# One number for a step's kind, read at the step's begin, in an attention and expert-routing kernel

## The chip, the cores and the metric

The kernel runs on one core of one Trainium2 chip. The metric is the device time of one execution in microseconds (us). The runs before the change took 690.76, 691.85 and 693.32 us, a median of 691.85 us.

A core has five engines that run their own instruction streams and meet at semaphores: PE (TensorE, the matmuls), DVE (VectorE), ACT (ScalarE), POOL (GpSimd) and SP (SyncE, which issues most transfers). A branch on a value that the kernel computed needs the value in a register of each engine that branches: the engine's stream holds an instruction TENSOR_LOAD that reads it from SBUF, and a compare-and-branch that uses it.

## The reference

A linear attention with random features over 8 batches of 576 tokens and 8 heads gives a matrix x of 4608 rows and 512 columns. Each row is then sent to one of 8 experts:

```python
logits = x @ w_gate
expert_idx = np.argmax(logits, axis=1)
...
for e in range(E):
    mask = expert_idx == e
    xe = x[mask]
    h = np.maximum(xe @ w1[e], 0.0)
    ye = h @ w2[e]
    out[mask] = gate_w[mask, None] * ye
```

`w1[e]` is 512 by 1024, `w2[e]` is 1024 by 512, all in float32. How many rows an expert gets is known only on the chip.

## The kernel before

The first 262 us or so are the attention. Its rows go to a buffer `token_rows` in HBM, and tables of row numbers are worked out on the chip (`slots`). `plan` (30-odd small DVE instructions on one partition) then fills `flags`, a table of integers with one column for a step: row 0 says that the expert changes, row 1 which expert to load next, row 2 that the step exists, row 4 that its second tile exists, and before the change row 5 that it has two tiles of 128 rows (a pair) and row 6 that its third tile has at most 64 rows (half).

The experts' part runs in steps. A step takes up to three tiles of 128 rows of one expert. Its rows are gathered from `token_rows` (`gather`, `gather3`: POOL), transposed by a transfer (`flips`, `flips3`: SP), put together as floats on ACT (`join`) and split in a high and a low part, `xh` by ACT and `xl` by DVE (`split_columns`). The first layer, `l1`, has three bodies of code: 256 columns for a pair, 320 where the third tile is half, 384 else. It stands twice, for the two halves of the hidden columns (`part` 0 and 1), and each half begins with the branches on the step's kind. A body makes groups of matmuls into a PSUM tile `p` (L1030); ACT writes `hh` from each (L1044) and DVE `hl` (L1045). The second layer, `l2`, multiplies `hh` and `hl` by the split `w2` (L1064 to L1066) for two or three tiles into `p_t`, `p_snu` and `p_skv`; `send` scales a tile with its gate on ACT and DVE (L1077, L1078), and POOL writes its rows out (L1079).

The order on each engine is the order in which the code is written (no scheduler moves it). In `step(t)` that is: `flips` of step t+1, the split of a new `w2` where the expert changes, `l1(t)`, the gathers of step t+2, the two loads of the kind of step t+1 (`kind`, by `reg` at L959: two on PE, DVE and ACT, one on POOL), `following`, and `l2(t)`. `following` is `begin(t+1)`: `xtrans` joins and splits the two tiles of the next step, `third` the third one, if the step is no pair (the branch at L1020 on `two`), and `change` splits a new `w1`. Steps from the 13th on stand in `tail`, nested, each under a branch on row 2.

A step begins with the first matmul of l1 on PE and has two borders there: from l1 to l2, where the two loads of the next step's kind stand, and from l2 to the next step's l1, where before the change there are branches alone (in `tail` the load of row 2, `v`, as well). The first step is led in by hand: the first two tiles of the table (`idx0`) are done in plain float32 by `l20(0)` and `l20(1)` (L933, into `p_snu` and `p_t`), and the kind of step 1 is loaded between those two.

```python
kind = self.kind(1)
self.third(kind[0])
...
self.l20(1)
...
for t in range(1, NPM - 1):
    kind = self.step(t, kind, ...)
```

Of the kernel before, what the change touches and what calls it, by code (L numbers as in the profile page):

```python
# [11 lines left out]
I32 = mybir.dt.int32  # L12
# [3 lines left out]
ALU = mybir.AluOpType  # L16
# [18 lines left out]
NPR = NPL + E - 1  # L35
NS = 3 * NPR
NPM = (NT // P - E) // 2
# [4 lines left out]
ET = mybir.EngineType  # L42
# [426 lines left out]
class Routing:  # L469
# [256 lines left out]
    def slots(self, wk, T1, banks, idx, fill, ahead):  # L726
# [14 lines left out]
        for c in (c1, c2, ch):  # L741
# [15 lines left out]
        nc.vector.scalar_tensor_tensor(out=v, in0=off, scalar=256.0, in1=m, op0=ALU.mult, op1=ALU.add)  # L757
        so, rt = self.L.rearrange("p g s e -> p (g s) e"), self.RT.rearrange("p g s -> p (g s)")
        y, tt, mv, sx, d, third, far = (t(n, [P, NLT]) for n in ("y", "tt", "mv", "sx", "d", "third", "far"))
        nc.vector.tensor_tensor(out=so, in0=self.OH.rearrange("p g s e -> p (g s) e"),  # L760
                                in1=v.unsqueeze(1).to_broadcast([P, NLT, E]), op=ALU.mult)
# [6 lines left out]
        nc.vector.scalar_tensor_tensor(out=d, in0=sx, scalar=64.0, in1=d, op0=ALU.mult, op1=ALU.add)  # L768
        nc.vector.scalar_tensor_tensor(out=mv, in0=d, scalar=-2.5, in1=sx, op0=ALU.is_gt, op1=ALU.mult)
        nc.vector.scalar_tensor_tensor(out=third, in0=d, scalar=-3.0, in1=sx, op0=ALU.is_equal, op1=ALU.mult)  # L770
        nc.vector.tensor_tensor(out=tt, in0=tt, in1=mv, op=ALU.subtract)
        nc.vector.scalar_tensor_tensor(out=third, in0=d, scalar=0.0, in1=third, op0=ALU.is_equal, op1=ALU.add)
# [22 lines left out]
    def plan(self, flags):  # L795


        nc, t, inc = self.nc, self.t, self.inc
# [20 lines left out]
        nt, en, sb = t("nt", [1, NQ]), t("en", [1, E]), t("sb", [1, NQ])  # L819
# [9 lines left out]
        sx, hf, two, thr = (t(n, [1, NQ]) for n in ("psx", "hf", "two", "thr"))  # L829
# [5 lines left out]
        nc.vector.scalar_tensor_tensor(out=two, in0=sb, scalar=4.0, in1=two, op0=ALU.is_equal, op1=ALU.add)  # L835
        nc.vector.tensor_tensor(out=two, in0=two, in1=sx, op=ALU.mult)
        nc.vector.scalar_tensor_tensor(out=two, in0=sb, scalar=3.0, in1=two, op0=ALU.is_equal, op1=ALU.add)
        nc.vector.tensor_single_scalar(flags[:, 5, :], two, 0.5, op=ALU.is_lt)
        nc.vector.scalar_tensor_tensor(out=flags[:, 6, :], in0=sb, scalar=5.0, in1=hf, op0=ALU.is_lt, op1=ALU.mult)
        nc.vector.tensor_single_scalar(flags[:, 4, :], sb, 1.5, op=ALU.is_gt)  # L840
        for i, a in ((0, ch), (1, nt), (2, act)):
            nc.vector.tensor_copy(flags[:, i, :], a)
# [2 lines left out]
class Experts:  # L845
# [6 lines left out]
    def __init__(self, tc, ctx, rt, xs, w1, w2, out, ident, ps):  # L852
        self.tc, self.nc, self.ctx, self.rt, self.ps, self.ident = tc, tc.nc, ctx, rt, ps, ident
        self.xs16, self.w1, self.w2, self.out = xs.bitcast(U16), w1, w2, out
        cp = ctx.enter_context(tc.tile_pool(name="mo_a", bufs=1))
        self.w1s = cp.tile([P, self.NC, F], F32, name="w1s")
        self.w2s = cp.tile([P, self.NF, DM], F32, name="w2s")
        self.idx = cp.tile([P, NS], U32, name="idx")
        self.x0 = cp.tile([P, self.NC, self.T2], F32, name="x0")
        self.idx0 = cp.tile([P, 2], U32, name="idx0")  # L860
        self.flags = cp.tile([1, 7, NPR + 2], I32, name="flags")
        self.xg = [cp.tile([P, 2 * ROW], U16, name=f"xg{i}") for i in range(2)]
        for x in self.xg:
            self.nc.gpsimd.memset(x, 0)
        rt.setup()
        rt.after[3] = rt.head(4, self.idx0, self.flags)
        gt = cp.tile([P, 8], F32, name="gt")
        self.gt = [gt[:, i:i + 1] for i in range(8)]
# [98 lines left out]
    def split(self, n, cs=range(8)):  # L967
        for c in cs:
            split_r(self.nc, *self.part(n, c), self.nc.scalar, self.nc.vector)
# [42 lines left out]
            self.split_columns(a, xw)  # L1012

    def flips3(self, t):
        with self.tc.If(self.reg(5, t, 1, (ET.SP,)) < 1):
            self.flip(self.xt3, self.x3)
        self.nc.gpsimd.tensor_copy(self.gt[6 + t % 2], self.gate(self.x3))

    def third(self, two):
        with self.tc.If(two < 1):  # L1020
            self.join(self.xw[0], self.xt3)
            self.split_columns(2, self.xw[0])

# [21 lines left out]
            self.nc.vector.scalar_tensor_tensor(out=b, in0=o, scalar=0.0, in1=a.bitcast(F32), op0=ALU.max,  # L1045
                                                op1=ALU.subtract)

    def l1(self, t, two, half):

        for part in range(2):  # L1050
            with self.tc.If(two > 0) as pair:
                self.layer(t, part, self.T2)
            with pair.Else():
                with self.tc.If(half > 0) as short:
                    self.layer(t, part, self.T2 + P // 2)
                with short.Else():
                    self.layer(t, part, self.T3)
# [36 lines left out]
        e = self.reg(1, t, E - 1, (ET.SP,))  # L1094
        (self.dma1 if n == 1 else self.dma2)(bass.ds(e, 1))

    def begin(self, t, kind):

        self.xtrans(t)
        self.third(kind[0])  # L1100
        self.change(t, 1)

    def kind(self, t):
        engines = (ET.PE, ET.DVE, ET.Activation, ET.Pool)
        return self.reg(5, t, 1, engines), self.reg(6, t, 1, engines[:3])

    def step(self, t, kind, following, split=lambda: None):
        engines = (ET.PE, ET.DVE, ET.Activation, ET.Pool)
        if t + 1 < NPR:
            self.flips(t + 1)  # L1110
            self.flips3(t + 1)
        split()
        two, half = kind
        self.l1(t, two, half)
        if t + 2 < NPR:
            self.gather(t + 2)
            self.gather3(t + 2)
        if t == 1:
            self.next(0, 2)
        kind1 = self.kind(t + 1) if t + 1 < NPR else None  # L1120
        following(kind1)
        self.nc.gpsimd.drain()
        with self.tc.If(two > 0) as pair:
            self.l2(t, 0)
            self.when(self.reg(4, t, 1, engines), lambda: self.l2(t, 1))
        with pair.Else():
            for a in range(3):
                self.l2(t, a)
        return kind1

    def tail(self, t, kind):
        split = lambda: self.change(t, 2)
        if t == NPR - 1:
            self.step(t, kind, lambda kind: None, split)
            return
        v = self.reg(2, t + 1, 1, (ET.PE, ET.DVE, ET.Activation, ET.SP, ET.Pool))
        kind = self.step(t, kind, lambda kind: self.when(v, lambda: self.begin(t + 1, kind)), split)
        with self.tc.If(v > 0):  # L1138
            self.tail(t + 1, kind)

    def run(self, ctx):
        nc, rt = self.nc, self.rt
        cp = ctx.enter_context(self.tc.tile_pool(name="mo_c", bufs=1))
        NC, NF, T2 = self.NC, self.NF, self.T2
        one, two = (self.ps.tile([P, 512], F32, name=f"p_s{g}", tag=g) for g in ("nu", "kv"))
# [35 lines left out]
        self.next(0, 1)  # L1181
        self.gather3(1)
        self.flips3(1)
        kind = self.kind(1)
        self.third(kind[0])
        self.gather(2)
        self.gather3(2)
        self.l20(1)
        self.hh, self.hl = held("hh"), held("hl")
        for t in range(1, NPM - 1):  # L1190
            kind = self.step(t, kind, lambda kind: self.begin(t + 1, kind), lambda: self.change(t, 2) if t > 1 else None)
        self.tail(NPM - 1, kind)


def attention_moe(tc, q, k, v, omega, wg, w1, w2, out, xs):
# [41 lines left out]
```

## Time and profile before

| what | value |
|---|---|
| runs, median | 690.76, 691.85, 693.32 us; 691.85 us |
| the profiled execution's own time | 687.46 us |
| its span, first to last instruction | 685.7 us |
| granted TensorE clock, mean | 0.997 |
| busy: PE, weight loads, ACT, DVE, POOL | 94%, 85%, 61%, 50%, 40% |
| steps of the experts' part | 15, the first matmul at 280.53, the last at 678.67 us |

The profile is of one execution. Times in its rows count from the first instruction. Register loads, branches and semaphore instructions are not in the rows as busy: what they cost is seen only as a time in which an engine begins its next instruction later than the one before would let it. A matmul row's duration overlaps the next row's (the matmuls are pipelined), so what a row takes of PE's time is the distance from its start to the next start.

### The profile page before, as it was taken

How to read it: one execution, taken by the hardware profiler on the slowest of the kernel's cores; microseconds unless marked ns; L12 is line 12 of the kernel's file. 1: busy time of each engine (PE TensorE's matmuls, PEld its weight loads, DVE VectorE, ACT ScalarE, POOL GpSimd, SP SyncE). 2: the span in 40 equal slices, each digit the busy share in tenths (PEclk: the TensorE clock that was granted, in tenths of full speed). 3: DMA queues.
4: the chain of work that ended last, by engine and by line, in shares of the span. 5: the costliest groups of instructions: out<-in, count | busy, mean ns of one | idle time of the engine just before them, and what ended most of it. 6: DMA issues, size and time to landing. Idle time of an engine off the chain costs nothing. (4 is left out here: it accounts for less than half of the span.)

```text
span 685.7 us, 19398 instructions
## 1 busy us (share of the span) xinstructions
PE 647.6 (94%) x7209; PEld 585.0 (85%) x7209; DVE 344.7 (50%) x800; ACT 416.3 (61%) x1037; POOL 277.7 (40%) x499
## 2 busy tenths in 40 slices
PE   6899999899899897999999999999999999999996
PEld 5788989889898884788998989988988989989894
DVE  3467979879888888622222245222245254222220
ACT  6999999999999986433424256134256264343320
POOL 8566767667668832523230303321203303312211
PEclk9999999999999999999999999999999999999998
DMA  7865475654834532694350119543219508732101
GB/s 214 223 193 163 120 211 152 198 155 128 233 118 157 179 90 62 213 208 126 86 111 17 64 48 290 128 72 74 64 56 267 145 6 278 191 68 50 43 8 38
DMA packets 113336, 89.93 MB, mean 131 GB/s; under 512 B 72222, under 2 KB 96798, under 8 KB 113184
## 3 DMA queue, kind: packets, MB, share of 16 engines
q1 hardware_dynamic: 105360, 68.78, 38.0%
q0 software_dynamic: 7280, 19.04, 8.2%
q8 instruction: 90, 1.47, 0.9%
q14 instruction: 62, 0.51, 0.3%
q10 hardware_dynamic: 544, 0.13, 0.1%
HBM read 63.46 MB, written 19.55 MB: 121 GB/s over the span
## 5 line engine op out<-in xcount | busy, mean ns | idle before, releaser
L1030 PE MATMUL p<-xh,w1p 128*128 128x256 f32 (+2 forms) x960 | 147.8, 296 | 0.0
L1079 POOL DMA_INDIRECT out_dram<-ys,idx x32 | 33.6, 1050 | 270.4 <-DVE ys L1078 194.2
L1030 PEld LDWEIGHTS p<-xh,w1p 128*128 128x128 f32 x960 | 135.3, 188 | 1.7 <-issue 0.5
L1044 ACT ACTIVATE hh<-p 128x384 fp32r<-128x384 f32 (+1 forms) x84 | 45.0, 537 | 131.2 <-PE p L1030 119.5
L1045 DVE SCALAR_TENSOR_TENSOR hl<-p,hh 128x384 fp32r<-128x384 f32 (+1 forms) x84 | 51.4, 614 | 122.8 <-ACT hh L1044 108.9
L233 ACT ACTIVATE qp<-pp,mx 128x128 f32<-128x128 f32 x256 | 94.6, 714 | 0.0
L233 ACT ACTIVATE kp<-pp,mx 128x128 f32<-128x128 f32 x256 | 92.2, 672 | 0.5 <-DVE mx L221 0.2
L221 DVE TENSOR_REDUCE mx<-pp 128x8 f32<-128x1024 f32 x64 | 78.0, 1219 | 26.2 <-PE pp L214 25.7
L1030 PE MATMUL p<-xl,w1p 128*128 128x256 f32 (+2 forms) x480 | 83.5, 296 | 0.0
L192 ACT COPY tq<-tt 128x1024 f32<-128x1024 f32 x59 | 81.5, 1381 | 0.9 <-PE tt L150 0.9
L214 PE MATMUL pp<-om_t,tq 64*128 64x128 f32 x1024 | 74.3, 284 | 2.6 <-ACT qp L233 1.7
L1030 PEld LDWEIGHTS p<-xl,w1p 128*128 128x128 f32 x480 | 70.5, 188 | 0.2 <-issue 0.2
L249 POOL TENSOR_TENSOR k<-kp 128x256 f32<-128x256 f32 x64 | 46.4, 725 | 54.0 <-ACT kp L233 50.4
L214 PEld LDWEIGHTS pp<-om_t,tq 64*128 64x128 f32 x1024 | 62.1, 187 | 6.3 <-ACT qp L233 3.2
L1004 ACT COPY xw<-xt 128x1024 uint16<-128x1024 uint16 x36 | 48.7, 1353 | 7.6 <-ACT hh L1044 4.5
L1064 PE MATMUL p_t<-w2p,hh 128*128 128x512 f32 x120 | 47.9, 399 | 4.4 <-ACT hh L1044 3.0
L48 DVE TENSOR_TENSOR xl<-xw,xh 128x512 fp32r<-128x512 f32 x36 | 24.8, 692 | 50.2 <-ACT xh L54 40.5
L305 PE MATMUL nu<-kva,tq 128*64 128x73 f32 x992 | 42.4, 230 | 5.4 <-ACT kva L292 5.4
L1065 PE MATMUL p_t<-w2p,hh 128*128 128x512 f32 x120 | 46.9, 391 | 0.3 <-issue 0.3
L1066 PE MATMUL p_t<-w2p,hl 128*128 128x512 f32 x120 | 47.1, 392 | 0.0
L1066 PE MATMUL p_snu<-w2p,hl 128*128 128x512 f32 x120 | 47.0, 391 | 0.0
L1064 PE MATMUL p_snu<-w2p,hh 128*128 128x512 f32 x120 | 47.0, 391 | 0.0
(395 smaller groups left out, 1281.3 us busy)
## 6 DMA issues: line engine op xcount, KB each, us to landing
w1s<-in_moe_w_dram SPq DMA_DIRECT2D x5, 2048.0 KB
w2s<-in_moe_w_dram SPq DMA_DIRECT2D x5, 2048.0 KB, 10.2
v<-in_v_dram SPq DMA_DIRECT2D x32, 256.0 KB, 3.5
token_rows<-xc SPq DMA_DIRECT2D x8, 1024.0 KB
k<-in_k_dram SPq DMA_DIRECT2D x31, 256.0 KB, 5.2
q<-in_q_dram SPq DMA_DIRECT2D x31, 256.0 KB, 5.6
kr<-in_k_dram SPq DMA_DIRECT2D x16, 64.0 KB, 3.7
vz<-in_v_dram SPq DMA_DIRECT2D x16, 64.0 KB, 2.4
```

The source lines that it names most:

```text
L192: self.nc.scalar.copy(self.pack(i, j), tt)
L214: nc.tensor.matmul(pp[:, a, n, i, :], th[r, k].rearrange("p a t -> p (a t)"), self.om[r, :], start=True, stop=True)
L221: nc.vector.tensor_reduce(out=mx[:, :, n], in_=s[("pp", h)][:, :, n], axis=AX.X, op=ALU.max, negate=True)
L233: nc.scalar.activation(x[:, j, :], pp[:, j % 2, n, j // 2, :], AF.Exp, bias=mx[:, j % 2, n, j // 2:j // 2 + 1])
L249: add = lambda o, x, y: nc.gpsimd.tensor_tensor(out=o, in0=x, in1=y, op=ALU.add)
L1004: self.nc.scalar.copy(x.bitcast(U16).rearrange("p c (t k) -> p k c t", k=2), xt.rearrange("p (k c) t -> p k c t", k=2))
L1030: self.nc.tensor.matmul(o, w[:, i, c], x[:, i, :], start=k == 0, stop=k == len(ops) - 1)
L1044: self.nc.scalar.activation(a, o, AF.Relu)
L1045: self.nc.vector.scalar_tensor_tensor(out=b, in0=o, scalar=0.0, in1=a.bitcast(F32), op0=ALU.max, op1=ALU.subtract)
L1064: nc.tensor.matmul(p, h, self.w2h[:, c, :], start=c == 0, stop=False)
L1065: nc.tensor.matmul(p, h, self.w2l[:, c, :], start=False, stop=False)
L1066: nc.tensor.matmul(p, l, self.w2h[:, c, :], start=False, stop=c == self.NF - 1)
```

## The change

The kind becomes one number in row 5: 2 for a pair, 1 for a half third tile, 0 else. It is loaded at three places, each time anew: by PE, DVE, ACT and POOL right before `l1(t)` (also used by the branch of `l2(t)`), by ACT and DVE in `third`, and by SP in `flips3` as before. The two loads between l1 and l2 are gone, and `third` is no branch of PE and POOL any more. `plan` has one instruction more.

```diff
-        nc.vector.tensor_single_scalar(flags[:, 5, :], two, 0.5, op=ALU.is_lt)
-        nc.vector.scalar_tensor_tensor(out=flags[:, 6, :], in0=sb, scalar=5.0, in1=hf, op0=ALU.is_lt, op1=ALU.mult)
+        nc.vector.scalar_tensor_tensor(out=hf, in0=sb, scalar=5.0, in1=hf, op0=ALU.is_lt, op1=ALU.mult)
+        nc.vector.tensor_scalar(out=two, in0=two, scalar1=-2.0, scalar2=2.0, op0=ALU.mult, op1=ALU.add)
+        nc.vector.tensor_tensor(out=flags[:, 5, :], in0=two, in1=hf, op=ALU.max)
...
-        self.flags = cp.tile([1, 7, NPR + 2], I32, name="flags")
+        self.flags = cp.tile([1, 6, NPR + 2], I32, name="flags")
...
-        with self.tc.If(self.reg(5, t, 1, (ET.SP,)) < 1):
+        with self.tc.If(self.kind(t, (ET.SP,)) < 2):
...
-    def third(self, two):
-        with self.tc.If(two < 1):
+    def third(self, t):
+        with self.tc.If(self.kind(t, (ET.DVE, ET.Activation)) < 2):
...
-            with self.tc.If(two > 0) as pair:
+            with self.tc.If(kind > 1) as pair:
                 self.layer(t, part, self.T2)
             with pair.Else():
-                with self.tc.If(half > 0) as short:
+                with self.tc.If(kind > 0) as short:
...
-    def kind(self, t):
-        engines = (ET.PE, ET.DVE, ET.Activation, ET.Pool)
-        return self.reg(5, t, 1, engines), self.reg(6, t, 1, engines[:3])
+    def kind(self, t, engines):
+        return self.reg(5, t, 2, engines)
...
         split()
-        two, half = kind
-        self.l1(t, two, half)
+        kind = self.kind(t, engines)
+        self.l1(t, kind)
...
-        kind1 = self.kind(t + 1) if t + 1 < NPR else None
-        following(kind1)
+        following()
         self.nc.gpsimd.drain()
-        with self.tc.If(two > 0) as pair:
+        with self.tc.If(kind > 1) as pair:
...
-        kind = self.kind(1)
-        self.third(kind[0])
+        self.third(1)
         self.gather(2)
         self.gather3(2)
         self.l20(1)
```

On PE, at the lead-in, before the change (`p_snu` is l20(0), `p_t` l20(1), `p<-xh,w1p` the first matmul of step 1):

```order
L933 MATMUL p_snu<-w2s,h_5983 128x512 x8
L959 TENSOR_LOAD flags
L959 ISA x2
L959 TENSOR_LOAD flags
L959 ISA x2
L1015 UNCONDITIONAL_BRANCH
L1020 COMPARE_AND_BRANCH
L1020 UNCONDITIONAL_BRANCH x2
L933 MATMUL p_t_5896<-w2s,h_5983 128x512 x3
L1015 UNCONDITIONAL_BRANCH
L933 MATMUL p_t_5896<-w2s,h_5983 128x512 x5
L1051 COMPARE_AND_BRANCH
```

The same place on PE in the changed kernel:

```order
L934 MATMUL p_snu<-w2s,h_5983 128x512 x8
L934 MATMUL p_t_5896<-w2s,h_5983 128x512 x8
L960 TENSOR_LOAD flags
L960 ISA x2
L1016 UNCONDITIONAL_BRANCH
L1021 UNCONDITIONAL_BRANCH
L1016 UNCONDITIONAL_BRANCH
L1052 COMPARE_AND_BRANCH
L1031 MATMUL p_5716<-xh,w1p_5723 128x256
```

The load has moved from between l20(0) and l20(1) to behind both, and there is one instead of two.

On PE, the border from l1 to l2 of step 1, before the change (the last matmuls of the 384 body, then the first of l2):

```order
L1030 MATMUL p_5719<-xl,w1p_5723 128x384 x4
L1054 UNCONDITIONAL_BRANCH
L959 TENSOR_LOAD flags
L959 ISA x2
L959 TENSOR_LOAD flags
L959 ISA x2
L1020 COMPARE_AND_BRANCH
L1020 UNCONDITIONAL_BRANCH x2
L1084 UNCONDITIONAL_BRANCH
L1123 COMPARE_AND_BRANCH
L1064 MATMUL p_t_5896<-w2p_5980,hh 128x512
```

In the changed kernel this border, with the border from l2 to the next step's l1 below it (from `p_skv` on):

```order
L1031 MATMUL p_5719<-xl,w1p_5723 128x384 x4
L1055 UNCONDITIONAL_BRANCH
L1021 UNCONDITIONAL_BRANCH
L1085 UNCONDITIONAL_BRANCH
L1122 COMPARE_AND_BRANCH
L1065 MATMUL p_t_5896<-w2p_5980,hh 128x512
...
L1067 MATMUL p_skv<-w2p_5980,hl 128x512
L1122 UNCONDITIONAL_BRANCH
L960 TENSOR_LOAD flags
L960 ISA x2
L1016 UNCONDITIONAL_BRANCH
L1085 UNCONDITIONAL_BRANCH
L1052 COMPARE_AND_BRANCH
```

The first border has lost both loads and one compare-and-branch; the second, which held two unconditional branches and the compare-and-branch, has got one load.

## Rows read from the trace of the kernel before

**Rows 1.** Groups by form on PE, 262 to 686: count | busy, mean | idle before

```profile
L1030 PE MATMUL p<-xh,w1p 128*128 128x256 f32 x576 | 78.2, 278 | 0.0
...
L1030 PE MATMUL p<-xh,w1p 128*128 128x384 f32 x192 | 37.5, 337 | 0.0
L1030 PE MATMUL p<-xh,w1p 128*128 128x320 f32 x192 | 32.0, 309 | 0.0
```

**Rows 2.** Waits of PE, 260 to 686: total us, times, longest

```profile
PE p_t L933 <- DVE w1p L48: 3.5, 1, 3.5
PE p_t L1064 <- ACT hh L1044: 3.0, 3, 1.2
PE p_t L1064 <- issue: 1.0, 3, 0.5
```

**Rows 3.** Timeline of PE, the lead-in: start us, duration us, instruction, count [idle before]

```profile
263.37 7.11 PE L933 MATMUL p_snu<-w2s,h 128*128 128x512 f32 x16
273.96 7.13 PE L933 MATMUL p_t<-w2s,h 128*128 128x512 f32 x16 [3.48 <-DVE w1p L48]
280.53 0.68 PE L1030 MATMUL p<-xh,w1p 128*128 128x256 f32 x1
```

**Rows 4.** Timeline of DVE at the same time

```profile
272.28 0.16 DVE L842 CAST flags<-f_act 1x27 int32<-1x27 f32 x1
272.36 2.48 DVE L48 TENSOR_TENSOR w1p<-w1s,w1p 128x512 fp32r<-128x512 f32 x4
...
275.17 1.27 DVE L48 TENSOR_TENSOR xl<-xw,xh 128x512 fp32r<-128x512 f32 x2
276.37 2.48 DVE L48 TENSOR_TENSOR w1p<-w1s,w1p 128x512 fp32r<-128x512 f32 x4
```

**Rows 5.** Timeline of PE, a pair's l1: between its halves, and its end

```profile
330.89 0.62 PE L1030 MATMUL p<-xl,w1p 128*128 128x256 f32 x4
331.34 1.07 PE L1030 MATMUL p<-xh,w1p 128*128 128x256 f32 x8
...
336.33 0.62 PE L1030 MATMUL p<-xl,w1p 128*128 128x256 f32 x4
336.98 0.47 PE L1064 MATMUL p_t<-w2p,hh 128*128 128x512 f32 x1
```

**Rows 6.** Timeline of PE, l1 to l2 of a 384 step and a 320 step

```profile
364.39 0.86 PE L1030 MATMUL p<-xl,w1p 128*128 128x384 f32 x4
365.09 0.39 PE L1064 MATMUL p_t<-w2p,hh 128*128 128x512 f32 x1
...
395.38 0.75 PE L1030 MATMUL p<-xl,w1p 128*128 128x320 f32 x4
396.20 0.47 PE L1064 MATMUL p_t<-w2p,hh 128*128 128x512 f32 x1
```

**Rows 7.** Timeline of PE, the longest gap between l1 and l2

```profile
468.63 0.62 PE L1030 MATMUL p<-xl,w1p 128*128 128x256 f32 x4
470.47 0.47 PE L1064 MATMUL p_t<-w2p,hh 128*128 128x512 f32 x1 [1.22 <-ACT hh L1044]
```

**Rows 8.** Timeline of ACT, from the last eviction of l1 to the next join

```profile
336.98 0.60 ACT L1044 ACTIVATE hh<-p 128x512 fp32r<-128x512 f32 x1 [2.07 <-PE p L1030]
337.92 1.36 ACT L1004 COPY xw<-xt 128x1024 uint16<-128x1024 uint16 x1 [0.34 <-ACT hh L1044]
```

**Rows 9.** Timeline of PE, from l2 to l1 in the tail, where a load stands

```profile
590.88 0.39 PE L1065 MATMUL p_snu<-w2p,hh 128*128 128x512 f32 x1
591.11 0.39 PE L1066 MATMUL p_snu<-w2p,hl 128*128 128x512 f32 x1
591.34 0.87 PE L1030 MATMUL p<-xh,w1p 128*128 128x256 f32 x6
```

**Rows 10.** Timeline, the last third tile on DVE and the l1 on PE that uses it

```profile
343.80 0.69 DVE L48 TENSOR_TENSOR xl<-xw,xh 128x512 fp32r<-128x512 f32 x1 [1.23 <-ACT xh L54]
...
348.13 0.34 PE L1030 MATMUL p<-xh,w1p 128*128 128x384 f32 x1
```

More of the change, by code (lines that the diff above doesn't have):

```diff
@@ L1046, in layer, with l1 @@
                                                 op1=ALU.subtract)
-    def l1(self, t, two, half):
+    def l1(self, t, kind):
         for part in range(2):
-            with self.tc.If(two > 0) as pair:
+            with self.tc.If(kind > 1) as pair:
                 self.layer(t, part, self.T2)
             with pair.Else():
-                with self.tc.If(half > 0) as short:
+                with self.tc.If(kind > 0) as short:
                     self.layer(t, part, self.T2 + P // 2)
@@ L1095, in next, with begin, step @@
         (self.dma1 if n == 1 else self.dma2)(bass.ds(e, 1))
-    def begin(self, t, kind):
+    def begin(self, t):
         self.xtrans(t)
-        self.third(kind[0])
+        self.third(t)
         self.change(t, 1)
-    def kind(self, t):
-        engines = (ET.PE, ET.DVE, ET.Activation, ET.Pool)
-        return self.reg(5, t, 1, engines), self.reg(6, t, 1, engines[:3])
-    def step(self, t, kind, following, split=lambda: None):
+    def kind(self, t, engines):
+        return self.reg(5, t, 2, engines)
+    def step(self, t, following, split=lambda: None):
         engines = (ET.PE, ET.DVE, ET.Activation, ET.Pool)
@@ L1128, in step, with tail @@
                 self.l2(t, a)
-        return kind1
-    def tail(self, t, kind):
+    def tail(self, t):
         split = lambda: self.change(t, 2)
         if t == NPR - 1:
-            self.step(t, kind, lambda kind: None, split)
+            self.step(t, lambda: None, split)
             return
         v = self.reg(2, t + 1, 1, (ET.PE, ET.DVE, ET.Activation, ET.SP, ET.Pool))
-        kind = self.step(t, kind, lambda kind: self.when(v, lambda: self.begin(t + 1, kind)), split)
+        self.step(t, lambda: self.when(v, lambda: self.begin(t + 1)), split)
         with self.tc.If(v > 0):
-            self.tail(t + 1, kind)
+            self.tail(t + 1)
     def run(self, ctx):
@@ L1183, in run @@
         self.flips3(1)
-        kind = self.kind(1)
-        self.third(kind[0])
+        self.third(1)
         self.gather(2)
@@ L1190, in run @@
         for t in range(1, NPM - 1):
-            kind = self.step(t, kind, lambda kind: self.begin(t + 1, kind), lambda: self.change(t, 2) if t > 1 else None)
-        self.tail(NPM - 1, kind)
+            self.step(t, lambda: self.begin(t + 1), lambda: self.change(t, 2) if t > 1 else None)
+        self.tail(NPM - 1)
 def attention_moe(tc, q, k, v, omega, wg, w1, w2, out, xs):
```

## The prediction

> **What bounds the kernel now.** I read first who PE waits for in the experts' part, since nothing else can move the end if PE is never idle there. The list of PE's waits from 260 us on is short: once 3.5 us in front of l20(1), and six times, 4.0 us in all, in front of the first matmul of l2 [rows 2]. So PE sets the time of this part, and a change of register loads counts only where PE starves: at the lead-in and at the borders between the layers. The groups by form say how many borders there are: a step has 64 matmuls of xh by w1, so 576, 192 and 192 of them are 9 pairs, 3 full steps of 384 columns and 3 of 320, 15 steps [rows 1].
>
> The timelines show what a border costs, by the distance between starts. Four 256-column matmuls take 0.45 us (330.89 to 331.34 [rows 5]). After the last four of a pair's l1, at 336.33, the next could begin at 336.78 and begins at 336.98: 0.20 lost, though no idle time is written in the row. In a 320 step four take 0.45 x 320/256 = 0.56; 395.38 makes 395.94, and 396.20 is 0.26 late. In a 384 step nothing is lost: 364.39 + 0.675 = 365.07 against 365.09 [rows 6]. The worst border loses 1.39 us: 468.63 + 0.45 = 469.08, and l2 begins at 470.47 [rows 7]; of these, 1.22 is its written idle time, so the restart adds about 0.2 to a written gap too. Over all of them: 4.0 written at six borders [rows 2] and about 0.2 at each of the 12 borders of pairs and 320 steps, 4.0 + 2.4 = 6.4 us.
>
> Two rows tell what makes these losses. Between the two halves of a pair's l1, PE also jumps over two unused bodies and takes the branch on the kind, yet with no load: 330.89 + 0.45 is 331.34, nothing lost [rows 5]. And the loss falls with the width of the matmuls that are still queued (0.20 to 0.26 at 256 and 320, 0.02 at 384). So PE's instruction stream works ahead by a certain queue of matmuls, and the two loads take a little more than a queue of narrow ones covers.
>
> **The change part by part.**
>
> Lead-in. Before, l20(1) stands behind the two loads, and these wait until DVE has written flags, at 272.28 + 0.16 = 272.44 [rows 4]. l20(0) starts at 263.37; l20(1) takes 280.53 - 273.96 = 6.57 from its start to the next instruction's, so l20(0) is through at 263.37 + 6.57 = 269.94, and l20(1), which reads nothing of flags, could start there instead of at 273.96 [rows 3]. The profile puts this wait down to a w1p instruction of DVE, which l20(1) does not use; by the order it is the flags. With the load behind l20(1), step 1 can begin at 269.94 + 6.57 = 276.51, 4.02 us earlier. What is late next: xl, written at 275.17 + 1.27 = 276.44, and the first half of the low part of w1, at 274.84 [rows 4]; plan's one instruction more (0.16 by its neighbours [rows 4], 0.2 with its wait) puts both later, xl to about 276.65. The matmuls on xl come behind the first eight, so they wait for nothing; the second half of w1, at 278.85 + 0.2, is wanted only by the second half of l1, more than 5 us into it. Bounds: 3.48 (only the written wait) to 4.02; I take 3.8.
>
> Border l1 to l2. Two loads, their four ISA instructions and one compare-and-branch go. The price of two loads has no row of its own. From above: flags are written at 272.44 and PE starts at 273.96, so two loads with a branch and the start cost at most 1.52 us [rows 3, 4]. From below: on ACT the two loads stand behind the last eviction, which starts at 336.98 and takes 0.60; the join starts at 337.92, so at least 0.34 is theirs, and 0.94 if they begin as the eviction does [rows 8]. I take 0.94, since there too the stream runs ahead under an instruction in execution. A border can give back no more than this. Three gaps are long (3.0 written [rows 2], 3.6 with the restart) and give 3 x 0.94 = 2.8; the other nine lose 1.0 + 9 x 0.2 = 2.8 and give it all: 5.6. With 0.34 a pair of loads, it is three times 0.34 for the long ones, the same for the three shorter written ones and 6 x 0.2 for the rest, 3.2; with 1.52 it is nearly all, 6.4. PE's code is shorter by some instructions in each step, so whatever makes three gaps long may fall on other borders: I take off one such gap, 1.0, and come to 4.6.
>
> [...]
>
> Border l2 to l1. One load is added on PE, behind 512-column matmuls. Before, the tail has a load at this very place (row 2 of flags, in front of step 13): 591.11 to 591.34 is 0.23, as 590.88 to 591.11 is, so it costs nothing [rows 9]. The cover is wide: 0.23 a matmul against 0.113 in a pair's l1. In the tail two loads now stand there; they cost 0.94 by the price above, and the queue that nearly covered two loads with 256-column matmuls covers twice that here. I take 0. From both sides: 0 to 0.94 for each of three borders of the tail, 2.8 at most; no gain, because nothing is lost there now.
>
> ACT and DVE. Each step they have two loads as before, one in front of l1, where ACT waits for PE (2.07 us before an eviction) [rows 8], and one in front of the third join instead of two in front of the first join. If it is all exposed, a third tile's xl comes up to 0.94 later and the first two up to 0.34 earlier. Today xl of a third tile ends at 343.80 + 0.69 = 344.49, and its l1 begins at 348.13: 3.6 us of slack [rows 10]. 0. POOL's load moves in front of l1 and SP's stays; the gathers are a whole step ahead. 0.
>
> Sum: 3.8 + 4.6 = 8.4 us. The profiled execution took 687.46 us (a span of 685.7 and 1.76 around it), so 679.06 for it; it lies 4.4 under the median of the runs, 691.85, which makes 683.45. I predict 683.5 us.
>
> **The rivals.**
>
> A. The border's losses stay: they are not the loads' but the jump's out of l1, when code must be fetched. For it: gaps of such different length (0 to 1.22 written) at places with the same instructions [rows 2, 7]. Against it: the jump between the halves of l1 loses nothing [rows 5]. Then only the lead-in is left: 691.85 - 3.8 = 688.0.
>
> [...]
>
> B. The lead-in's wait comes back at step 1: l1 waits for the whole of DVE's low part of w1, 278.85 + 0.2 [rows 4]. For it: DVE has its queue full until then. Against it: the halves are separate instructions, and only the first is used at first. Gain 280.53 - 279.05 = 1.5 instead of 3.8: 691.85 - 1.5 - 4.6 = 685.75.
>
> C. Both gains are lost in the pipeline: 15 steps later, transfers or evictions that were just in time are late by what PE has won, and the time is that of no change within 0.5%, some 690. For it: slack at one step's border need not be there at all fifteen. Against it: the 3.6 us at the one that is shown [rows 10], and PE waits for no transfer [rows 2].
>
> D. Slower. The new load in front of l1 is not covered: PE's stream reaches it only when l2's queue has run down, and each of the 15 borders pays for a load. It decides from (8.4 + 3.5)/15 = 0.8 us a border; with the 1.52 of above it costs 15 x 1.52 = 22.8, and the time is 691.85 - 8.4 + 22.8 = 706. Against it stands the tail's border with a load and no loss [rows 9].
>
> **How the numbers follow.** Forecast (both gains) 0.55, A 0.17, B 0.10, C 0.13, D 0.05. A measurement tells no change from about 0.5%, 3.46 us here. The forecast and B are faster by more; A, at 3.8, is so in about half of its cases: 0.55 + 0.10 + 0.09 = 0.74, and with a C that loses only a part, 0.76. Same: the rest of A and C, 0.19. Slower: D, 0.05. The forecast alone spans the bounds 3.48 + 3.2 = 6.7 to 4.02 + 6.4 = 10.4, so 681.4 to 685.2. The range takes in B and A: 681.0 to 689.0.
>
> **What would show it.** Right: no gap between `p_snu` and `p_t` of L933's successor, step 1 beginning near 276.6, 15 borders from l1 to l2 with under 0.1 each, the other border still 0.23 a start, and PE's waits for `p_t` nearly gone. Wrong: written idle time of PE in front of the first matmul of l1 (D, or B at step 1 alone), gaps of 0.5 to 1.2 still in front of l2 (A), or waits for xt, xh or xl in later steps (C).

## The result and the profile after

The changed kernel took 684.27 us (median of 682.27, 682.38, 686.16 and 686.56), the kernel before beside it 691.31 us (690.41 to 693.32): a ratio of 0.9895, with a 95% interval from 0.9848 to 0.9943. On another chip, later on, it took 686.69 us (682.02 to 688.41, 12 runs) against 689.32 us, a ratio of 0.9956 (0.9935 to 0.9977). It is faster on both, by 7.0 us on the first and by 2.6 on the second; the 2.6 alone would lie within the 0.5% that the prediction called no change. The forecast was 683.5 us.

The profiled execution took 686.16 us (span 684.1), that of before 687.46 us (685.7). PE's waits in the experts' part come first, as they did for the kernel before [rows 2]: who waited for whom, total us, times, longest.

```profile
PE p L1031 <- ACTq L1085: 1.0, 1, 1.0
PE p L1031 <- DVEq L1085: 0.6, 1, 0.6
PE p_skv L787 <- DVE f_T L780: 0.3, 1, 0.3
```

The waits for `p_t` are gone, the one in the lead-in and the six in front of l2. In their place stand two waits of l1 (L1031, the old L1030), both at one step. The timeline of PE at the lead-in (start, duration, instruction, count) answers to [rows 3]:

```profile
264.10 7.11 PE L934 MATMUL p_snu<-w2s,h 128*128 128x512 f32 x16
271.04 7.03 PE L934 MATMUL p_t<-w2s,h 128*128 128x512 f32 x16
277.51 1.51 PE L1031 MATMUL p<-xh,w1p 128*128 128x256 f32 x8
```

From the start of l20(0) to the first matmul of step 1 it is 277.51 - 264.10 = 13.41 us, before 280.53 - 263.37 = 17.16: 3.75 less, and l20(1) begins 6.94 behind l20(0), with no gap. The borders, again on PE's timeline, answer to [rows 5 to 7] and, at the end, to [rows 9]:

```profile
337.54 0.63 PE L1031 MATMUL p<-xl,w1p 128*128 128x256 f32 x4
338.01 0.39 PE L1065 MATMUL p_t<-w2p,hh 128*128 128x512 f32 x1
...
365.31 0.87 PE L1031 MATMUL p<-xl,w1p 128*128 128x384 f32 x4
366.01 0.40 PE L1065 MATMUL p_t<-w2p,hh 128*128 128x512 f32 x1
...
469.31 0.64 PE L1031 MATMUL p<-xl,w1p 128*128 128x256 f32 x4
469.79 0.39 PE L1065 MATMUL p_t<-w2p,hh 128*128 128x512 f32 x1
...
589.54 0.39 PE L1067 MATMUL p_snu<-w2p,hl 128*128 128x512 f32 x1
589.77 0.40 PE L1031 MATMUL p<-xh,w1p 128*128 128x256 f32 x2
```

From the last four matmuls of l1 to l2 it is 0.47 to 0.48 in a pair and 0.70 at 384 columns, four starts and nothing more; the border that lost 1.39 us [rows 7] has nothing left to lose (469.31 to 469.79). From l2 to l1 it is 0.23, as before [rows 9].

Adding such distances from start to start over the whole experts' part, stage by stage, gives a ledger of each profiled execution. "Fastest" is the third kernel of experiment 5, put beside them here.

| us | before | after | difference | fastest |
|---|---|---|---|---|
| start of l20(0) (attention, routing) | 263.37 | 264.10 | +0.73 | 263.30 |
| lead-in: l20(0) to step 1 | 17.16 | 13.41 | -3.75 | 13.41 |
| l1, 15 steps | 192.41 | 199.65 | +7.24 | 192.29 |
| 15 borders l1 to l2 | 6.36 | 0.0 | -6.4 | 0.06 |
| l2, 15 steps | 199.55 | 198.06 | -1.49 | 198.12 |
| 14 borders l2 to l1 | 0.06 | 1.19 | +1.13 | 0.06 |
| behind l2, to the span's end | 6.8 | 7.7 | +0.9 | 7.7 |

So both gains that the prediction named came, the second one larger: 3.75, and 6.4 + 1.5 at the borders and right behind them. But 8.4 us went elsewhere: l1 itself got slower, and one border from l2 to l1 has a wait. Neither stands in the prediction's sum.

**The wait is at step 2.** PE's timeline there, in the changed kernel:

```profile
300.15 0.40 PE L1067 MATMUL p_snu<-w2p,hl 128*128 128x512 f32 x1
301.51 0.38 PE L1031 MATMUL p<-xh,w1p 128*128 128x256 f32 x1 [0.97 <-ACTq L1085]
302.52 1.48 PE L1031 MATMUL p<-xh,w1p 128*128 128x256 f32 x7 [0.63 <-DVEq L1085]
303.80 1.05 PE L1031 MATMUL p<-xl,w1p 128*128 128x256 f32 x4
304.66 1.91 PE L1031 MATMUL p<-xh,w1p 128*128 128x256 f32 x8
306.36 0.68 PE L1031 MATMUL p<-xl,w1p 128*128 128x256 f32 x4
```

PE waits twice, and then eight matmuls take 1.70 (304.66 to 306.36), where the next pair's take 0.96 (329.38 to 330.34, shown further down). The busy times by stretch tell why (stretch and length, busy us of PE, its weight loads, DVE, ACT, POOL, then the granted clock as a share of full speed, DMA share, GB/s):

```profile
298.00:301.51 3.51, 2.55 (x12) 1.75 (x10) 1.36 (x2) 2.44 (x3) 2.31 (x4) 1.00 0.80 228
301.51:304.00 2.49, 1.86 (x9) 1.66 (x10) 0.99 (x3) 0.95 (x2) 0.00 (x0) 0.80 1.03 338
304.00:306.00 2.00, 2.00 (x12) 2.00 (x11) 0.00 (x0) 0.00 (x0) 0.00 (x0) 0.50 0.96 325
306.00:308.00 2.00, 2.00 (x17) 2.00 (x17) 0.17 (x1) 0.60 (x1) 0.17 (x1) 0.89 1.15 274
```

After the waits the granted clock fell to 0.50 (304 to 306 us) and was at 0.89 in the stretch from 306 to 308. Step 2 began 1.1 us late, and its l1 took 14.01 us against 11.51 of the next pair: 0.9 of these 2.5 us are the second wait (301.51 to 302.52, where a start takes 0.12) and 1.6 the lower clock, 3.6 in all. The wait starts 25 us earlier on POOL, in the changed kernel:

```profile
276.37 4.24 POOL L1080 DMA_INDIRECT out_dram<-ys,idx  x1 [8.44 <-DVE ys L1079]
280.61 1.19 POOL L1012 COPY gt<-xgm 128x1 f32<-128x1 f32 x2
281.95 1.08 POOL L983 DMA_INDIRECT x<-token_rows,idx  x1
288.95 0.36 POOL L1018 COPY gt<-x 128x1 f32<-128x1 f32 x1 [5.92 <-DMA x<-token_rows,idx]
289.66 1.03 POOL L983 DMA_INDIRECT xg<-token_rows,idx  x1 [0.36 <-issue]
```

and in the kernel before:

```profile
275.52 1.23 POOL L1079 DMA_INDIRECT out_dram<-ys,idx  x1 [8.32 <-DVE ys L1078]
276.74 0.95 POOL L1011 COPY gt<-xgm 128x1 f32<-128x1 f32 x2
277.84 1.36 POOL L982 DMA_INDIRECT x<-token_rows,idx  x1 [0.15 <-POOL gt L1011]
280.37 0.18 POOL L1017 COPY gt<-x 128x1 f32<-128x1 f32 x1 [1.17 <-DMA x<-token_rows,idx]
281.85 1.03 POOL L982 DMA_INDIRECT xg<-token_rows,idx  x1 [1.30 <-issue]
```

The first row store took 4.24 instead of 1.23 us. Behind it on POOL stands the gather of step 1's third tile (`x`), and with that delay it went out at 281.95, after SP had issued the 2 MB load of w1 at 279.85; before, it went out at 277.84, ahead of that load (279.00). POOL waited 5.92 us for it instead of 1.17, so the next step's gathers went out 8 us later than before (289.66 against 281.85), and with them came ACT's join and DVE's xl of step 2. The late store is only half of the cause: experiment 2 has it too, in a kernel whose PE comes later, and no wait.

**l1 is slower in every pair.** Four 256-column matmuls took 0.45 us from start to start in a pair of before (330.89 to 331.34 [rows 5]). In the same pair of after, on PE's timeline, the four on xl take 0.48 (330.34 to 330.82):

```profile
329.38 1.12 PE L1031 MATMUL p<-xh,w1p 128*128 128x256 f32 x8
330.34 0.64 PE L1031 MATMUL p<-xl,w1p 128*128 128x256 f32 x4
330.82 1.12 PE L1031 MATMUL p<-xh,w1p 128*128 128x256 f32 x8
```

A start is 113.3 ns behind the last in most pairs of before (118 in two, and one changes from 113 to 118 in its middle), and 120.0 ns in all nine of after. Over the nine pairs and the 384 steps that is 4.7 us, which with the 2.5 of step 2 makes the 7.24 of the ledger. The instructions are the same ones. What differs is where their data lie: `flags` shrank from 7 to 6 rows of integers, in the allocation from 768 to 672 bytes, and every tile allocated behind it moved down by 96 bytes: xh, which these matmuls stream, from 148672 to 148576 in its partition, a multiple of 64 before and not after. w1 did not move.

### The profile page after: what moved, and what is told of

It reads as the page before. It is cut to its first block, busy times and chain, and to the rows that moved or that the text cites. A ratio compares the mean times of both kernels' runs of the same rounds, so it can differ in the third digit from the quotient of the medians.

```text
span 684.1 us, 19349 instructions
## 1 busy us (share of the span) xinstructions
PE 651.1 (95%) x7209; PEld 591.0 (86%) x7209; DVE 345.6 (51%) x801; ACT 415.9 (61%) x1037; POOL 281.5 (41%) x499
## 5 line engine op out<-in xcount | busy, mean ns | idle before, releaser
L1031 PE MATMUL p<-xh,w1p 128*128 128x256 f32 (+2 forms) x960 | 152.5, 301 | 1.6 <-ACTq L1085 1.0
L1031 PEld LDWEIGHTS p<-xh,w1p 128*128 128x128 f32 x960 | 139.1, 190 | 3.9 <-ACTq L1085 1.4
L1080 POOL DMA_INDIRECT out_dram<-ys,idx x32 | 36.5, 1140 | 252.0 <-DVE ys L1079 177.4
L1031 PE MATMUL p<-xl,w1p 128*128 128x256 f32 (+2 forms) x480 | 85.5, 300 | 0.0
L1031 PEld LDWEIGHTS p<-xl,w1p 128*128 128x128 f32 x480 | 72.3, 190 | 0.0
```

The source lines that it names most:

```text
L1031: self.nc.tensor.matmul(o, w[:, i, c], x[:, i, :], start=k == 0, stop=k == len(ops) - 1)
```

## The experiments

Each kernel ran beside the kernel before, on one chip per group of runs.

**1. The table at seven rows.**

```diff
-        self.flags = cp.tile([1, 6, NPR + 2], I32, name="flags")
+        self.flags = cp.tile([1, 7, NPR + 2], I32, name="flags")
```

> The changed kernel with its flags tile kept at seven rows, as before the change (the seventh is not used), so that every tile that is allocated behind it keeps the address it had before. Theory 1 (the addresses of the moving operands set the pitch of the pair matmuls): the start-to-start pitch of the 256-column l1 matmuls goes from 120.0 ns in the changed kernel back to about 113 ns, which is 9 pair steps x 96 x 6.7 ns = 5.8 us less; with the steps that were at 118 ns before the change perhaps only 4 to 5 us; time 676 to 680 us. Theory 2 (what the engines load in front of l1 sets the pitch): the loads are those of the changed kernel, so the pitch stays at 120 ns and the time at 682 to 686.5 us.

Measured: 682.63 us (679.11 to 684.04), ratio 0.9886 (0.9847 to 0.9924). The pitch (the distance from start to start) is back: 113.4 to 113.6 ns in five pairs and 118 in four. So addresses, not loads, set it. The median lies above the expected 676 to 680 us. The profiled execution (684.04 us) has the stall of step 2 in a worse form, a loss of 3.1 us in front of it and then matmuls at 213 ns under a granted clock of 0.50 (304 to 308 us); whether the other three had it is not shown. The size had to wait for a run without the stall.

**2. The kernel before, with its tiles moved by 32 bytes.**

```diff
         self.flags = cp.tile([1, 7, NPR + 2], I32, name="flags")
+        cp.tile([P, 8], F32, name="shift")
```

> The kernel before the change with an unused tile of 32 bytes per partition allocated behind the flags, so that the tiles behind it move by 32 bytes and the moving operands of l1 begin 32 bytes off a multiple of 64, as in the changed kernel; no instruction changes. Theory 1 (addresses): the pair matmuls go from 113 to 120 ns, 9 x 96 x 6.7 ns = up to 5.8 us more, less what the steps at 118 ns already lose: 695 to 697.5 us. Theory 2 (the loads in front of l1): 113 ns as before and 690 to 693 us.

Measured: 692.09 us, ratio 1.0028 (1.0005 to 1.0051), so 0.3 to 3.5 us slower, under the 4.4 to 6.9 expected. The pitch is 118.3 ns in all nine pairs, not 120, and 173.5 at 384 columns, where it was 174.7 to 176.7; l1 sums to 194.80 us against 192.41. An unused tile of 32 bytes, and no other change, makes the kernel slower: the direction holds, the size was too high.

This profiled execution also shows what the late store costs when PE comes later. From POOL, DVE and PE:

```profile
277.75 4.23 POOL L1080 DMA_INDIRECT out_dram<-ys,idx  x1 [8.31 <-DVE ys L1079]
...
302.95 0.69 DVE L48 TENSOR_TENSOR xl<-xw,xh 128x512 fp32r<-128x512 f32 x1 [1.22 <-ACTq L1021]
...
307.41 0.76 PE L1031 MATMUL p<-xh,w1p 128*128 128x256 f32 x5
```

The store takes 4.23 us with the instructions of the kernel before, and POOL waits 5.50 us for the gather. But xl of step 2 is ready at 302.95 + 0.69 = 303.64 and step 2 begins at 307.41, so PE does not wait there. Of these 3.8 us of slack a lower clock in the lead-in gave 1.7 (experiment 6). The changed kernel's lead-in is shorter by 3.75 us at the full clock and has no such slack.

**3. Only the lead-in.** The kernel before, with l20(1)'s matmuls moved and nothing else (`l20` got an argument that says which part to issue):

```diff
+        self.l20(1, (0,))
         kind = self.kind(1)
...
-        self.l20(1)
+        self.l20(1, (1,))
```

> The kernel before the change with only one part of the change: the 16 matmuls of the second stored tile, l20(1), issued ahead of the loads and branches of the lead-in; the flags, the loads and the border l1 to l2 stay as they were. The prediction's lead-in step: TensorE goes from l20(0) into l20(1) without a gap, 3.5 to 4.0 us less, so 687 to 689 us, with the border losses (6.4 us in 15 borders) as before. Rival B (the wait comes back at step 1): gap in front of step 1 instead, and less than 2 us gained, 689.5 us or more.

Measured: 685.78 us, ratio 0.9950 (0.9929 to 0.9970), 2.1 to 4.9 us less. The lead-in takes 13.41 us as in the changed kernel, and the borders lose 6.4 as before. The store of the first rows took 1.23 us here and step 2 waited for nothing: PE's early start alone makes no stall either. Rival B falls.

**4. Loads back at the border.** Experiment 1's kernel with two unused loads, no branch:

```diff
+        if t + 1 < NPR:
+            for _ in range(2):
+                self.reg(5, t + 1, 2, (ET.PE,))
         following()
```

> The first experiment's kernel (flags at seven rows) with two unused register loads on TensorE's queue between l1 and l2 of each step, about what the change took out there (without the branches). The prediction's border step (TensorE's queue runs out behind the last l1 matmuls while it loads): the 15 borders lose again, most at 256 columns, where the run-ahead of some 17 matmuls covers 1.9 us and two loads take 1.4 us and more with what stands around them: 0.5 to 6.4 us more than the first experiment's kernel; gaps in front of l2 of 0 to 0.5 us in the pair steps. Rival A (the border losses were the fetch of code and not the loads): no gaps in front of l2 and the same time as the first experiment's kernel within 0.5 us.

Measured: 685.51 us, ratio 0.9931 (0.9903 to 0.9958), 2.9 us over experiment 1's median on the same chip, inside the expected 0.5 to 6.4. By stage the borders lose 4.7 us where experiment 1 loses nothing, and l2 takes 199.93 us against 198.07. PE's timeline at two of them:

```profile
335.11 0.62 PE L1031 MATMUL p<-xl,w1p 128*128 128x256 f32 x4
335.56 0.39 PE L1065 MATMUL p_t<-w2p,hh 128*128 128x512 f32 x1
...
523.44 0.63 PE L1031 MATMUL p<-xl,w1p 128*128 128x256 f32 x4
525.09 0.47 PE L1065 MATMUL p_t<-w2p,hh 128*128 128x512 f32 x1 [1.01 <-ACT hh L1045]
525.40 0.40 PE L1066 MATMUL p_t<-w2p,hh 128*128 128x512 f32 x1
```

The first loses nothing, the second 1.20 us, and l2's first start distance is 0.31 instead of 0.23, which is how a border's gap runs on into l2 (the larger part of the 1.86 us in l2, 1.08, stands in step 6 alone, 12.03 against 10.95). The trace also has records of the register instructions, which the views leave out. On PE a load takes 0.30 us, and 0.69 until the next one can start; the stream is some 33 instructions (16 to 17 matmuls with their weight loads) ahead of the matmul in execution, 1.9 us of 256-column ones. Two loads at 0.69 fit into that. At the five pair borders that lost (0.47 to 1.45 us) something took longer: a load of 0.63 to 0.87 us, a branch of 1.73 in the first step, or, at 522.36, 1.5 us of nothing behind a load. So the loads use up the cover and an irregular delay then shows; without the loads (experiment 1, same branches) it shows at no border.

The quiet borders' 0.2 does not come back: steps 2, 3, 5, 6, 11 and 12 lose 0.00 to 0.06 here. At the border of [rows 5], in the kernel before, the records run from 335.00 to 336.93, 1.92 us, for two loads and three branches; here (333.78 to 335.33) two loads and one branch take 1.54. So that part of the loss was of loads and branches together, and two loads alone, without the branches, bring back 4.7 of 6.4.

As the account of all the borders rival A (the jump alone) falls, since experiment 1 has the jumps and no loss. Whether the delays are fetches of code stays open. The trace's packets of an instruction queue (q8, 16 KB each) overlap four of the five delays and begin just behind the fifth (445.06, where the slow load ended at 444.99); there is none at the quiet borders of steps 3, 5, 6 and 12, but there is one at those of steps 2 and 11. Whose code they bring is not recorded.

**5. The changed kernel again, the early gather, and both with the old addresses** (on one chip):

```diff
         self.gather(1)
+        self.gather3(1)
         self.flips(1)
...
         self.third(1)
         self.gather(2)
-        self.gather3(1)
         self.gather3(2)
```

The sketch is of the second kernel; the third has the seven rows of experiment 1 as well.

> The changed kernel once more, on the chip of the next runs, for the comparison with them: 682 to 687 us. Its first row store on POOL either takes 1.2 us (then no stall at step 2, about 682 us) or 4.2 us (then the stall at step 2 costs 3 to 4 us, about 686 us).

> The changed kernel with one move on POOL's queue: the gather of the third tile's rows of step 1 is issued right behind the gather of its pair, ahead of SP's first 2 MB load of w1 and of the first row store; tiles and everything else as in the changed kernel (pair pitch 120 ns). Theory (rival C of the prediction, at one place: a late gather behind the 2 MB load delays step 2): the wait of l1 of step 2 on ACT and DVE goes, step 2 starts at 120 ns from its first matmuls, and the time is 0 to 4 us under the changed kernel's, 681 to 683 us steadily, with less spread. Rival (the stall comes from something else, as the lead-in being shorter by 3.75 us with DVE and ACT the limit): the wait stays and the time is that of the changed kernel.

> As the run before (gather of the third tile moved ahead) and with the flags tile at seven rows besides, so that the tiles behind it have the addresses of before the change. Theory (addresses set the pitch): the pair steps are at 113 ns but for two or three at 118 ns, 6 x 96 x 6.6 ns + 3 x 96 x 2.2 ns = 4.4 us less than the run before, 676 to 679 us, the fastest of all. If the step-2 stall were independent of the gather, 680 us and more.

| us | median (range), runs | ratio to before (95%) | l1 | borders l2 to l1 |
|---|---|---|---|---|
| changed kernel again | 686.69 (682.02 to 688.41), 12 | 0.9956 (0.9935 to 0.9977) | 199.97 | 1.55 |
| early gather | 683.94 (682.02 to 684.48), 6 | 0.9912 (0.9890 to 0.9934) | 197.14 | 0.06 |
| early gather, seven rows | 678.44 (676.62 to 679.11), 5 | 0.9840 (0.9817 to 0.9863) | 192.29 | 0.06 |

With the gather early, the store takes 4.24 us as in the changed kernel, but the gather is out before it, and POOL's next copy waits for nothing:

```profile
269.98 1.01 POOL L983 DMA_INDIRECT x<-token_rows,idx  x1 [0.30 <-issue]
278.12 4.24 POOL L1080 DMA_INDIRECT out_dram<-ys,idx  x1 [7.13 <-DVE ys L1079]
282.36 1.19 POOL L1012 COPY gt<-xgm 128x1 f32<-128x1 f32 x2
283.50 0.17 POOL L1018 COPY gt<-x 128x1 f32<-128x1 f32 x1
```

The stall is gone and its price is 2.8 us on the median (686.69 - 683.94); the intervals of the two ratios do not overlap, and 683.94 is 0.9 above the expected 681 to 683. The addresses are worth 5.5 us more (683.94 - 678.44), of which 4.85 show in l1. In the third kernel PE waits for no one from 262 us to the end: its list of waits is empty. Its 678.44 lies in the expected 676 to 679. That version beats both kernels: by its interval it is 1.4 to 1.8% faster than the kernel before.

**6. One load back in the lead-in**, in the fastest kernel above:

```diff
+        self.reg(5, 1, 2, (ET.PE,))
         self.l20(1)
```

> The kernel of the run before with one unused register load of the flags on TensorE's queue between l20(0) and l20(1), where the change took two loads and a branch out. Theory (the lead-in's wait is the flags' arrival, and the loads only add to it): one load alone brings most of it back; flags done about 1.3 us behind l20(0)'s end, 0.7 us for the load, some 0.5 us until the next matmul: a gap of 2.4 to 3.2 us between l20(0) and l20(1), and 2.4 to 3.2 us on the time. Rival (the two loads and the branch were the wait, 0.7 to 1 us each): a gap of under 1.2 us.

Measured: 681.89 us in one run, 3.45 over that kernel's median. PE's timeline and the busy times by stretch (as above, the clock behind POOL's):

```profile
274.04 8.82 PE L934 MATMUL p_t<-w2s,h 128*128 128x512 f32 x16 [2.69 <-DVE w1p L48]
282.29 0.93 PE L1031 MATMUL p<-xh,w1p 128*128 128x256 f32 x3
```

```profile
271.18:274.04 2.86, 0.17 (x2) 0.01 (x1) 2.59 (x17) 1.81 (x2) 0.00 (x0) 1.00 0.78 144
274.04:276.00 1.96, 1.96 (x3) 0.96 (x4) 1.96 (x4) 1.92 (x3) 0.00 (x0) 0.62 0.03 8
276.00:278.00 2.00, 2.00 (x4) 0.70 (x3) 2.00 (x5) 0.55 (x1) 1.50 (x1) 0.52 0.00 0
278.00:280.00 2.00, 2.00 (x6) 0.93 (x5) 1.83 (x4) 0.00 (x0) 2.00 (x1) 1.00 0.00 0
```

l20(0) starts at 264.24 and takes 6.94, so the gap is 274.04 - 271.18 = 2.86 us, inside the 2.4 to 3.2. Most of it is the flags' arrival: DVE writes their last row until 273.43, 2.25 us behind l20(0), and l20(1) begins 0.61 after that. With the two loads and the branch of the kernel before it began 1.52 after them (272.44 to 273.96 [rows 3, 4]), so the loads add to the wait but are the smaller part. And the clock fell behind it, to 0.62 and 0.52, so that l20(1) took 282.29 - 274.04 = 8.25 us instead of 6.5: the lead-in is 18.06 instead of 13.41. In the profiled execution of before the clock stayed at 1.00 behind a gap of 3.65 us; in that of experiment 2, with the same instructions and a gap of 3.63, it fell (0.50 from 277 to 279 us) and the lead-in took 18.83. So the lead-in's gap was worth 3.75 us in the one and 5.4 in the other; how often either happens is not shown.

**7. Six loads from l2 to l1**, in the fastest kernel:

```diff
         split()
+        for _ in range(6 if t > 1 else 0):
+            self.reg(5, t, 2, (ET.PE,))
         kind = self.kind(t, engines)
```

> The fastest version so far (third tile's gather moved ahead, seven-row flags table) with six unused register loads on TensorE's queue in front of the load of the kind, at each border from l2 to l1 of steps 2 to 15 (14 borders). The prediction took the l2-to-l1 border as covered, since TensorE's queue runs ahead of its matmuls there by more than the chain of the load takes. Theory (the run-ahead is some 33 instructions, that is 16 to 17 matmuls of 512 columns, 3.8 us by the trace; the chain is 1.15 us, and six loads at 0.69 us make it 5.3 us): a gap of about 1.4 us at each of the 14 borders, 18 to 24 us more than that version. [...]

Measured: 716.04 us in one run, 37.6 over the fastest kernel's median, which is from another chip. All 14 borders lose, 1.19 to 2.92 us, 25.1 in all; a typical one on PE's timeline:

```profile
322.37 0.40 PE L1067 MATMUL p_snu<-w2p,hl 128*128 128x512 f32 x1
324.17 1.07 PE L1031 MATMUL p<-xh,w1p 128*128 128x256 f32 x7 [1.40 <-ACTq L1085]
```

The queue runs ahead by about 33 instructions at this border too, as the theory had it, and the one load of the change (a chain of 1.15 us under a cover of 3.8) lies well inside. The expected 18 to 24 was too low for these borders already, and there was more: the granted clock fell to 0.50 four times behind a gap, and three borders from l1 to l2, where no load stands, lost 5.1 us (0.25, 2.92 and 1.95). The worst of these on PE's timeline:

```profile
426.19 0.62 PE L1031 MATMUL p<-xl,w1p 128*128 128x256 f32 x4
429.57 0.77 PE L1065 MATMUL p_t<-w2p,hh 128*128 128x512 f32 x1 [2.76 <-ACT xh L54]
```

The trace's records have one compare-and-branch of PE there that lasts 4.64 us, and one of 3.75 at the other, each with a packet of the instruction queue q8 inside. So a jump without a load can outlast the cover. In the nine other profiled executions without loads at this border none of the 135 lost more than 0.15 us, with branches of up to 1.9 us.

**8. Which address?** Three lengths of the unused tile in front of xh, six-row table, early gather. w2, hh and hl stay where the changed kernel has them.

```diff
-        cp.tile([P, 48], F32, name="pad1")
+        cp.tile([P, 72], F32, name="pad1")
```

(72, 56 and 40 columns in the three kernels.)

> The kernel with the third tile's gather moved ahead and the flags table at six rows, with the unused tile in front of xh made 96 bytes longer: xh and xl (which l1's matmuls stream) and what lies behind them are back at their addresses of before the change, while w2p, hh and hl stay 96 bytes lower. Theory 1a (the address of the operand that streams decides the pitch): pair steps at 113 ns, but for those that were at 118 ns with all tiles in place. Theory 1b (it is another tile's address): 120 ns in all pair steps, as with the six-row table alone.

> As the run before, with that unused tile 32 bytes longer instead of 96: xh at 148608, a multiple of 64 (and of 128), but not its address of before the change (148672, a multiple of 64). Theory 1c (what counts is that the streamed operand begins on a multiple of 64 bytes): 113 to 118 ns in the pair steps and 676 to 680 us. Theory 1d (what counts is the place itself, for instance against other tiles'): 118 to 120 ns in all pair steps and 682 to 685 us.

> As the run with the longer tile, with the unused tile in front of xh 32 bytes shorter than in the changed kernel: xh at 148544, which is 128 bytes below its address of before the change (so the same within 128 bytes, and a multiple of 64), where 148608 (a multiple of 64 as well) gave 118 to 120 ns. Theory 1e (the place within 128 bytes counts): 113 ns in most pair steps, some at 118 as with xh at 148672, and 678 to 681 us. Theory 1f (only that one place, or a relation to more tiles, is good): 118 to 120 ns in all pair steps and 681 to 685 us.

Mean distance from start to start by kernel, in ns, from the matmuls' records (step 1 and the steps with a fallen clock by their later matmuls):

```
xh at    kernels                        pairs                                       384 columns
148672   before, exps. 1, 4, fastest    113.3 in most, 117.8 in two to four          174.7 or 176.7
148672   tile of 72                     113.6 in six, 117.8 in three                 176.7
148704   before, moved by 32 bytes      118.3 in all                                 173.5
148608   tile of 56                     118.6 in seven, 120.0 in two                 175.5 to 176.0
148576   changed kernel, early gather   120.0 in all                                 176.7
148544   tile of 40                     117.8 in all                                 173.3
```

The tile of 72 gave 679.98 us in one run, that of 56 681.32 (680.20 to 682.59, ratio 0.9872, 0.9842 to 0.9902), that of 40 679.79 in one run. 1b falls: putting xh and xl (and what lies behind) back is enough, with w2, hh and hl still moved. 1c falls too: 148608 is a multiple of 64 and gives 118.6. 1e falls: 148544 is the same place within 128 bytes and gives 117.8. These verdicts go by the paces; the times agree less well (681.32 is just under the 682 to 685 of 1d, and 679.79, in one run, lies in the 678 to 681 of 1e). What is left is that the address of what TensorE streams (or of a tile behind it, which moved along), or its relation to the weights' that stay fixed, decides among five paces from 113.3 to 120.0 ns at 256 columns, and ranks them in another order at 384; at 320 all have 146.7 where no gap falls into the step. No rule for it came out, nor why steps of one kernel differ by 4.5 ns. The address is not all: in step 10 of the kernel before the pace went from 113 to 118 ns within one step, behind two late starts (257 and 226 ns).

## Why the prediction came out as it did

**Lead-in.** Right: 3.75 for 3.8. Experiment 3, with this edit alone, measured 2.1 to 4.9, and nothing came back at step 1 (B, at 0.10). The upper bound of 4.02 took 6.57 us for l20(0) as for l20(1); it takes 6.94 (264.10 to 271.04). What it missed: the clock can fall behind the gap, as in experiment 2, which costs 1.7 more in an execution where it does.

**Border l1 to l2.** The mechanism was right in kind and the term undersized: 4.6, measured 6.4 at the borders and 1.5 in l2 behind them. Three sizes were off. Two loads were taken at 0.94, the nearest row of another engine, and as the most that a border can give back; PE's own records have 0.69 for each load and 1.92 with the branches around them, and the three longest borders gave back 1.39, 1.10 and 0.99. 1.0 was taken off for a long gap that would fall on another border; none did in the changed kernel (0.00 to 0.01 at all 15). And nothing was put for l2. Experiment 4 shows the loads at work only where something else was late too. A, at 0.17, falls as the account of these borders, yet two jumps of experiment 7 lost 2.92 and 1.95 us without a load.

**Border l2 to l1.** Right, 0.00 at 13 of 14, and experiment 7 shows the reserve. D, at 0.05, falls.

**Transfers late by what PE has won.** This was C, put as an end of all gain with 0.13, for "slack at one step's border need not be there at all fifteen". It happened at one step, for 3.6 us in the profiled execution and 2.8 on the median. It takes two things together. A row store on POOL takes 3 us longer and a gather falls behind a 2 MB load; and PE, early by what the lead-in has won, comes before the data. With the late store and the late PE (experiment 2), and with the early PE and the short store (experiment 3), nothing waits; with the early gather (experiment 5) nothing waits either. The prediction put POOL at 0 with "the gathers are a whole step ahead", which the gather of the first step's third tile is not. What makes the store long is not shown; the change does not decide it alone, since the kernel before has it too when its tiles move by 32 bytes.

**What no term stood for.** The diff's one line on the table's size, which the prediction does not mention. It cost 4.7 us of the 8.4 forecast (5.5 by experiment 5).

So 683.5 against 684.27 is luck in good part: two terms right in kind, one 3.3 us too small, against two losses of 3.6 and 4.7 us that the sum did not have. The ledger of the two profiled executions ends at -1.6 us on the span; the medians' -7.0 is more, and on the other chip -2.6. The executions of both kernels spread by several us (687.11 to 695.91 and 682.02 to 688.41 over all chips); the fall of the clock in the lead-in and the stall of step 2 are two things that the traces show in some profiled executions, and how much of the spread is theirs is not shown.

## What to carry to other kernels

A change of control flow also moves data, if it resizes a table that is allocated ahead of the operands (here by 96 bytes, with 113.3 ns a start before and 120.0 after): compare the addresses and the pace of the same matmuls before the gain is counted, and keep the old size when in doubt. A register load cost nothing here while the engine's stream was further ahead than the load and the branches around it take (1.15 us under 3.8 us of 512-column matmuls, where two loads and three branches, 1.92 us, lost 0.2 behind 256-column ones), so put it behind wide matmuls rather than between narrow ones. When an engine's lead-in is shortened, look for the transfers on POOL and SP that can be late at no cost until then, such as a gather that must go out ahead of a large load (2.8 us here).

## What the runs showed of the hardware

- The pace of a 256-column matmul of one shape and type took values from 113.3 to 120.0 ns when the tiles from its streamed operand on were moved, by steps of 32 bytes among others; 384-column ones from 173.3 to 176.7.
- The first store of rows on POOL took either 1.23 us (the kernel before, experiment 3, the tile of 56 columns) or 4.23 to 4.24 (the eleven other profiled executions), with DVE's passes in the same order. In the changed kernel the long store ended 0.91 us behind DVE's four passes over w1 (277.22 + 2.48 = 279.70, and 276.37 + 4.24 = 280.61); the other 37 stores of rows in that execution took 0.97 to 1.54. This could mean that the store waited for the passes, but the 1.23 us store of the kernel before (275.52 to 276.75) ran beside passes of the same kind (275.17 to 278.85), and no run took DVE's passes away: the cause is not shown.
- Behind waits of PE (0.97 and 0.63 us at step 2, a gap of 2.86 in experiment 6, one of 3.63 in experiment 2) the granted clock was 0.50 to 0.62 over stretches of 2 to 4 us, and 1.00 behind the gap of 3.65 in the kernel before [rows 3].
- PE's stream ran 16 to 17 matmuls ahead of the one in execution, 1.9 us of 256-column ones and 3.8 of 512-column ones (experiments 4 and 7).
